# Ten transfers instead of sixteen per attention chunk, and an earlier start of attention, in a fused gated attention and MLP kernel

## The chip, the cores and the metric

The kernel runs on one core of a Trainium2 chip, as one launch. The metric is the device time of that launch in microseconds (us). PE is the matrix engine, DVE the vector engine, ACT the scalar engine, POOL the GpSimd engine and SP the engine whose queue issues the transfers (DMAs) between DRAM and on-chip memory. Every transfer of this kernel is issued from SP.

## The reference

Both branches read the same `x` (2048 rows of 512). Branch A is causal attention with 32 heads of 16 and a window of 256 keys; branch B is a dense MLP with 1792 hidden columns and tanh gelu. A sigmoid gate per row mixes them. All is float32.

```python
def _A_ref(x, wqkv, wo):
    B, S, D = x.shape
    H = 32; Dh = D // H; W = 256
    qkv = (x @ wqkv).reshape(B, S, 3, H, Dh)...      # q, k, v by head
    scores = einsum("bhqd,bhkd->bhqk", q, k) * Dh ** -0.5
    mask = (q - k >= 0) & (q - k < W)
    o = einsum("bhqk,bhkd->bhqd", softmax(where(mask, scores, -1e9)), v)
    return o.reshape(B, S, D) @ wo

def _B_ref(x, w1, b1, w2, b2):
    return gelu(x @ w1 + b1) @ w2 + b2

g = sigmoid((x * gate_w).sum(-1, keepdims=True))
out = g * a + (1 - g) * b
```

(The code is shortened; `a` and `b` are the two branches on `x`.)

## The kernel before

**Number format.** Each float32 operand is split into a high part, rounded to the narrower type `F32R`, and a low part that is the rest. A dense product is then three matmuls (high by high, high by low, low by high; `mm3`, lines 92 to 95). In attention the parts are stacked instead: one head of q or k becomes 48 partitions (16 dimensions by 3 copies), so that one matmul does the three products at once. These stacks (`ks`, `kd` for k, `qs`, `qd` for q) are why q and k go out to DRAM after the projection (tensors `SQ`, `SK`) and come back in another arrangement.

**Dense work.** The sequence is cut into four tiles of 512 rows (`T`). For each tile, `qkv` transposes x (`qkv_x`), makes eight pieces of q and k (`qkv_qk`, 128 columns, that is eight heads, each) and four of v (`qkv_v`), and stores them. After the four tiles come eight turns of the MLP (`mlp`), each on one tile and half of the hidden columns: first layer (matmuls `u`, with `gelu`), then second layer (matmuls `y`, partial sums to and from DRAM in `YA`, `YB`). Last comes `final`, the product with `wo` and the gate. While a tile of the MLP is worked on, its x is read back from `XT`.

**Attention.** Heads go in eight groups of four (`NG`), and a group in 16 blocks of 128 rows (`NKB`), four blocks to a chunk. So there are 128 block steps, 32 chunks. For step `u` the main loop (lines 785 to 812) issues, in four rounds,

- `att_max` for the block that is `LEAD` steps ahead: matmul `sm` (line 424, from `qd` and `kd`) and a row maximum on DVE (line 429);
- `att_exp`: matmul `st` (line 467, from `ks` and `qs`), the exponential on ACT (line 482), the triangular masks on POOL (lines 473, 476);
- `att_pvs` once per chunk: the matmuls `pv` with v (line 504), the sum of its two halves into the tile `nd` (lines 525, 528) and the store of `nd` to `ND` (line 529);
- `fill`: dense matmuls taken from the generator above, worth `STEP` (or `STEP0` before step 0) nanoseconds by a written cost per matmul triple.

So the dense work lies between the attention matmuls on PE, all in one order written ahead of time. `after(ns, fn)` puts a follow-up step into that order at a written delay; `need(key)` runs such steps until the key is there. Dense work worth `START` is put ahead of the first attention step.

**The loads of a chunk.** `ks`, `kd` and `qd` have two slots each and are refilled chunk by chunk: `load_qd` (four transfers, line 395), `load_kd` (one, line 387), `att_load_v` (three, lines 408 and 410), `load_ks` (six, lines 378, 379, 381) and `load_qs` (two, line 401). The first three are called at the end of the first block step of a chunk, `load_ks` at the end of the second, `load_qs` at the end of the third.

**The queue.** The orders of PE, ACT, DVE and POOL are as written. SP's order is set by the scheduling layer from the same program. SP works strictly in order: a transfer that waits for its data or for its buffer holds up all transfers behind it. Beside that, every transfer in the built program waits for the transfer eight places before it, because eight completion counters are used in turn; so at most eight are under way.

Of the kernel before, what the change touches and what calls it, by code (L numbers as in the profile page):

```python
# [32 lines left out]
def gated_mix(ctx: ExitStack, tc: tile.TileContext, x, wqkv, wo, w1, b1, w2, b2, gate_w, out):  # L33
# [90 lines left out]
    def load_raw(key, early=False):  # L124
# [15 lines left out]
        nc.sync.dma_start(raw.rearrange("p (c f) -> p c f", c=NC) if len(src.shape) == 3 else raw, src)  # L140
# [40 lines left out]
    def clear_k(i):  # L181

        pr, n = divmod(i, 2)
        for s in range(2):
            v = of_head(ks[:, pr, n], s)
            nc.scalar.activation(v, nil.unsqueeze(2).unsqueeze(3).broadcast_to([128, 4, 2, 64]), AF.Identity,
                                 bias=own[:, 2 * pr + s:2 * pr + s + 1])
# [57 lines left out]
    def qkv_qk(t, j):  # L245

        xt = xts[t]
        dst, i = (SQ[t], j) if j < NC else (SK[:, :, :, t * T:(t + 1) * T], j - NC)
# [18 lines left out]
        after(100, hi), after(700, lo)  # L267

    def qkv_v(t, b):
# [11 lines left out]
        def ev():  # L281
            to = vx[:, :, 0:16].rearrange("p (g s a) d -> p g a s d", s=2, a=2)
            for s in range(2):
                nc.scalar.activation(to[:, :, :, s], p.rearrange("p (g a s d) -> p g a s d", a=2, s=2, d=16)[:, :, :, s],
                                     AF.Copy)
            nc.sync.dma_start(SV[t][ts], vx)
# [10 lines left out]
    def qkv(t):  # L297
# [3 lines left out]
        pieces = qk[:2] + vs + qk[2:] if last else qk + vs  # L301
# [13 lines left out]
        for n, (kind, j) in enumerate(pieces):  # L315
# [17 lines left out]
            if t == 2 and n in (1, 3, 5, 7):  # L333
                clear_q(n // 2)
# [12 lines left out]
            if last and n not in (4, 5):  # L347
                load(later.pop(0))
# [15 lines left out]
    def parts(st, g_, cols):  # L364

        return st[4 * g_:4 * g_ + 4, :, :, cols].rearrange("(a s) d u c -> s (d u) a c", s=2)

    def load_ks(g_, c):


        need(("qk", c, NC + g_ // 2))
        src = parts(SK, g_, slice(c * T, (c + 1) * T))
        for pr in range(2):
            for s in range(2):
                v = f32(ks[64 * s + 4:64 * s + 52, pr, slot(g_, c)]).rearrange("r (n u j) -> r n u j", u=4, j=64)
                w = src[s, :, pr].rearrange("r (n u j) -> r n u j", u=2, j=64)
                if s:
                    nc.sync.dma_start(v[:, :, 0], w[:, :, 0])
                    nc.sync.dma_start(v[:, :, 3], w[:, :, 1])
                else:  # L380
                    nc.sync.dma_start(v[:, :, 1:3], w)

    def load_kd(g_, c):
        need(("qk", c, NC + g_ // 2))
        k0 = max(c * T - W, 0)
        src = SK[4 * g_:4 * g_ + 4, :, :, k0:(c + 1) * T].rearrange("(a s) d u c -> (s d u) a c", s=2)
        nc.sync.dma_start(f32(kd[0:96, :, slot(g_, c), k0 - c * T + W:]), src)

    def load_qd(g_, c):
        need(("qk", c, g_ // 2))  # L390
        src = parts(SQ[c], g_, slice(0, T))
        for pr in range(2):
            for s in range(2):
                v = f32(qd[48 * s:48 * s + 48, pr, slot(g_, c)]).rearrange("r (n s j) -> r n s j", s=2, j=64)[:, :, s]
                nc.sync.dma_start(v, src[s, :, pr].rearrange("r (n j) -> r n j", j=64))

    def load_qs(g_, c):
        need(("qk", c, g_ // 2))
# [464 lines left out]
```

## Time and profile before

| | |
|---|---|
| time, median of 3 runs | 806.6 us (804.92 to 808.64) |
| the profiled execution | 806.2 us, of which the span in the trace is 804.5 us |
| PE busy | 755.9 us, 94% of the span |
| PEld (weight loads, beside PE) | 616.2 us, 77% |
| DVE, ACT, POOL busy | 510.1, 432.8, 422.7 us (63%, 54%, 53%) |
| mean granted PE clock | 0.975 of full speed |
| transfers by SP's queue | 208400 packets, 174.91 MB, 78.6% of 16 DMA engines' time |

A row of waits reads: engine, line, who released it, then total us, times, and the longest. A timeline row reads: start, duration, engine, line, instruction, count, and in brackets how long the engine had been idle before and what ended that. In a row of windows, an engine's busy time is followed by its instruction count; PEclk is the clock granted to PE as a share of full speed, and it is followed by the share of the DMA engines' time that was busy and by GB/s. "SPq" is SP issuing a transfer; the transfer lands later.

### The profile page before, as it was taken

To read this page: it belongs to the slowest core of one execution; us is meant where nothing else is said; L and a number is where in the kernel's file an instruction comes from. 1 tells how busy PE (TensorE), PEld (TensorE's weight loads), DVE (VectorE), ACT (ScalarE), POOL (GpSimd) and SP (SyncE) were. 2 spreads that over 40 slices of the span, in tenths; PEclk is the share of its full clock that TensorE was granted. 3 is DMA by queue.
4 is the path that set the end of the run, shared out by engine and by line. 5 is a ranking of instruction groups with operands and counts; after the bars stand their busy time and mean duration, and the time that the engine had idled before them with its cause. 6 is when DMAs were issued, how large, how long until landed. Compare 5 with 4: busy or idle time off the path is not lost.

```text
span 804.5 us, 18387 instructions
## 1 busy us (share of the span) xinstructions
PE 755.9 (94%) x6102; PEld 616.2 (77%) x6102; DVE 510.1 (63%) x1548; ACT 432.8 (54%) x941; POOL 422.7 (53%) x1129
## 2 busy tenths in 40 slices
PE   9999999969999989989999797999978999999988
PEld 6888888848788868868777676788856887878776
DVE  4433333869579648856985597569646875793533
ACT  4434423357468427735873485458624853785541
POOL 3200000139669747856776387569844885687200
PEclk9999999989999989999999899999989999999999
DMA  9997988978977787888858888676787888758572
GB/s 301 402 332 275 358 271 268 297 155 281 213 178 188 202 201 183 241 205 185 181 145 217 229 197 238 172 175 136 216 209 174 191 232 198 184 154 250 171 245 104
DMA packets 208494, 176.09 MB, mean 219 GB/s; under 512 B 126480, under 2 KB 150288, under 8 KB 208400
## 3 DMA queue, kind: packets, MB, share of 16 engines
q1 hardware_dynamic: 208400, 174.91, 78.6%
q8 instruction: 49, 0.80, 0.5%
q14 instruction: 45, 0.37, 0.2%
HBM read 112.47 MB, written 62.39 MB: 217 GB/s over the span
## 4 chain that ended last, share of the span: by engine, by line
PE 68%; DMA 20%; DVE 5%; issue 2%; SPq 2%; POOL 1%; ACT 1%; DVEq 0%; POOLq 0%
PE pv_sm L504 7%; PE st L467 6%; PE sm L424 6%; DMA ks<-SK 6%; PE u L93 5%; PE u L95 4%; PE u L94 4%; DMA kd<-SK 4%; PE y L93 4%; PE qk L93 4%; PE qk L95 4%; PE qk L94 4%; PE y L94 4%; PE y L95 4%; DMA qd<-SQ 2%
## 5 line engine op out<-in xcount | busy, mean ns | idle before, releaser
L482 ACT ACTIVATE pt<-st 128x320 f32<-128x320 f32 (+4 forms) x512 | 207.8, 425 | 170.5 <-PE st L467 164.8
L429 DVE CUSTOM_DVE_ANT_0 jm<-sm,mask 128x320 bf16<-128x320 f32 (+4 forms) x512 | 237.5, 464 | 91.5 <-PE sm L424 67.1
L473 POOL TENSOR_SCALAR_AFFINE_SELECT pt<-pt 64x128 f32<-64x128 f32 x512 | 186.7, 365 | 178.3 <-ACT pt L482 157.1
L467 PE MATMUL st<-qs,ks 128*128 128x320 f32 (+4 forms) x512 | 159.5, 315 | 21.3 <-DMA ks<-SK 19.6
L424 PE MATMUL sm<-kd,qd 96*128 96x320 f32 (+4 forms) x512 | 158.2, 311 | 14.5 <-DMA kd<-SK 10.3
L476 POOL TENSOR_SCALAR_AFFINE_SELECT pt<-pt 64x128 f32<-64x128 f32 x448 | 152.4, 340 | 0.0
L467 PEld LDWEIGHTS st<-qs,ks 128*128 128x128 f32 x512 | 99.0, 193 | 46.8 <-issue 21.6
L424 PEld LDWEIGHTS sm<-kd,qd 96*128 96x128 f32 x512 | 98.0, 191 | 43.1 <-DVE M L429 13.5
L450 POOL CAST qs<-tt 4x512 fp32r<-4x512 f32 x128 | 90.2, 705 | 46.2 <-DVE tt L444 38.9
L95 PE MATMUL y<-w,h 128*128 128x512 f32 x224 | 89.7, 400 | 1.7 <-DVE h L619 1.7
L93 PE MATMUL y<-w,h 128*128 128x512 f32 x224 | 91.1, 407 | 0.0
L94 PE MATMUL y<-w,h 128*128 128x512 f32 x224 | 89.8, 401 | 0.0
L93 PE MATMUL u<-mx,w 128*128 128x512 f32 x196 | 81.3, 415 | 0.0
L504 PE MATMUL pv_sm<-pt,vbuf 64*32 64x320 f32 (+4 forms) x1408 | 77.5, 358 | 2.8 <-DVE M L429 2.4
L94 PE MATMUL u<-mx,w 128*128 128x512 f32 x196 | 78.2, 399 | 0.0
L95 PE MATMUL u<-mx,w 128*128 128x512 f32 x196 | 78.1, 399 | 0.0
L504 PE MATMUL pv_st<-pt,vbuf 64*32 64x320 f32 (+4 forms) x1408 | 77.0, 358 | 0.6 <-POOL pt L473 0.6
L504 PEld LDWEIGHTS pv_sm<-pt,vbuf 64*32 64x32 f32 x1408 | 53.0, 110 | 23.6 <-issue 4.0
L262 DVE TENSOR_TENSOR qke<-qk,qke 128x512 fp32r<-128x512 f32 x32 | 22.1, 691 | 49.0 <-ACT qke L259 42.8
L95 PEld LDWEIGHTS y<-w,h 128*128 128x128 f32 x224 | 43.0, 192 | 11.9 <-DVE h L619 2.1
L259 ACT ACTIVATE qke<-qk 128x512 fp32r<-128x512 f32 x32 | 19.2, 599 | 57.1 <-PE qk L95 40.1
L504 PEld LDWEIGHTS pv_st<-pt,vbuf 64*32 64x32 f32 x1408 | 49.0, 110 | 0.9 <-POOL pt L473 0.9
(140 smaller groups left out, 1330.5 us busy)
## 6 DMA issues: line engine op xcount, KB each, us to landing
kd<-SK SPq DMA_DIRECT2D x24, 576.0 KB
qd<-SQ SPq DMA_DIRECT2D x128, 96.0 KB
qs<-SQ SPq DMA_DIRECT2D x64, 192.0 KB
mx<-XT SPq DMA_DIRECT2D x24, 512.0 KB
SQ<-qke SPq DMA_DIRECT2D x16, 512.0 KB
SK<-qke SPq DMA_DIRECT2D x16, 512.0 KB
ND<-nd SPq DMA_DIRECT2D x32, 256.0 KB
raw_w<-in_B_w_dram SPq DMA_DIRECT2D x28, 256.0 KB
```

Of the source, the lines that this page charges most:

```text
L93: nc.tensor.matmul(p, lh, rh, start=first, stop=False)
L94: nc.tensor.matmul(p, lh, rl, start=False, stop=False)
L95: nc.tensor.matmul(p, ll, rh, start=False, stop=last)
L262: nc.vector.tensor_sub(e[:, 1 - h], p, f32(e[:, h]))
L424: nc.tensor.matmul(p[:, :w], qd[0:96, pr, n, 128 * j:128 * (j + 1)], kd[0:96, pr, n, k1 - w:k1], start=True, stop=True)
L429: nc.vector.tensor_tensor_reduce(junk[:, :w], p[:, :w], mask[:, 320 - w:320], 1.0, -3e38, ALU.add, ALU.max, M[:, 2 * (b % RB) + hb, pr:pr ...
L450: nc.gpsimd.tensor_copy(dst, tt[32 * i:32 * i + 4].unsqueeze(1).broadcast_to([4, 2, 2 * RB, 32]))
L467: nc.tensor.matmul(p[:, :w], ks[:, pr, slot(g_, kb // NB), at:at + 128], qs[:, pr, k0:k0 + w], start=True, stop=True)
L473: nc.gpsimd.affine_select(out=v[:, :, 0:64], in_=v[:, :, 0:64], pattern=[[0, 2], [1, 64]], compare_op=ALU.is_ge, fill=0.0, base=0, channel ...
L476: nc.gpsimd.affine_select(out=v[:, :, W:W + 64], in_=v[:, :, W:W + 64], pattern=[[0, 2], [-1, 64]], compare_op=ALU.is_ge, fill=0.0, base=- ...
L482: nc.scalar.activation(pt[:, pr, :w], p[:, :w], AF.Exp, scale=SCALE)
L504: nc.tensor.matmul(pv[r // 64][32 * i:32 * i + 32, q - c * T:e - c * T], vts[g_, b // NB][r:r + 64, v:v + 32], rhs(r), start=start, stop=s ...
```

## The change

1. **Layout in DRAM.** `SQ` and `SK` are stored as [8, 16, 3, 4, T]: the four pieces of 128 columns lie side by side, innermost but for the row. A group of four heads is now two neighbouring heads of two neighbouring pieces, and its two pairs lie side by side in DRAM and in the chip's `ks`, `qd`, `kd`. `SK` is one tensor per tile and not one for all. `SV` is stored already shifted by half a block for one of its halves.
2. **Fewer loads.** `load_ks` has 3 transfers (was 6), `load_qd` 2 (was 4), `att_load_v` 1 (was 3), `load_qs` 2 as before; `load_kd` has 2, where it was 1, for all chunks but the first of a group, since the rows of the tile before come from another tensor. That is 10 in place of 16. The stores of v are 3 per block where they were 1.
3. **Order of the loads.** `load_ks` is called one block step earlier (the first of a chunk), `load_qd`, `load_kd` and `att_load_v` one later (the second).
4. **`HOLD`.** The stores of q, k, v, `nd` and of the second layer's partial sums are put 1.5 us later in the written order than the instruction that makes their data.
5. **Start.** Attention begins after 90 us worth of dense work (was 117), in the third tile, with `LEAD` 12 (was 8); `STEP0` is 3000 (3150), `STEP` 2422 (2296). Weight loads are paced at 5 us (4). The last tile makes four q and k pieces ahead of its v pieces (two before).

```diff
-    SQ = [dr.tile([H, 16, 3, T], F32, name=f"SQ{t}") for t in range(NT)]
-    SK = dr.tile([H, 16, 3, S], F32, name="SK")
-    SV = [dr.tile([T, H, 17], F32, name=f"SV{t}") for t in range(NT)]
+    SQ = [dr.tile([H // NC, 16, 3, NC, T], F32, name=f"SQ{t}") for t in range(NT)]
+    SK = [dr.tile([H // NC, 16, 3, NC, T], F32, name=f"SK{t}") for t in range(NT)]
+    SV = [dr.tile([128, NB, 2, H // 2 * 17], F32, name=f"SV{t}") for t in range(NT)]
...
-            to = dst[8 * i:8 * i + 8].rearrange("h d s c -> (h d) s c")
+
+        def store():
+            to = dst[:, :, :, i].rearrange("h d s c -> (h d) s c")
             nc.sync.dma_start(to[:, 0:2], f32(e))
             nc.sync.dma_start(to[:, 2], f32(e[:, h]))
             done.add(("qk", t, j))
-        after(100, hi), after(700, lo)
+        after(100, hi), after(700, lo), after(700 + HOLD, store)
...
-            nc.sync.dma_start(SV[t][ts], vx)
+            nc.sync.dma_start(SV[t][:, b, 1], flat[:, n:2 * n])
+            for r in (0, 64):
+                nc.sync.dma_start(SV[t][64 - r:128 - r, b, 0], flat[r:r + 64, 0:n])
...
-            if t == 2 and n in (4, 6):
-                load_ks(0, n // 2 - 2)
-            if t == 2 and n in (9, 10):
-                load_kd(0, n - 9)
+            if t == 2 and n in (1, 2):
+                load_kd(0, n - 1)
+            if t == 2 and n in (8, 9):
+                load_ks(0, n - 8)
...
     def load_ks(g_, c):
...
+        ready(c, g_, 1)
+        n = 2 * NB
+        for s in range(2):
+            v = f32(ks[64 * s + 4:64 * s + 52, slot(g_, c)]).rearrange("r a x -> r (a x)")
+            src = part(SK[c], g_, s)
+            if s:
+                mid = v[:, 192:192 + 256 * (n - 1)].rearrange("r (n x) -> r n x", x=256)[:, :, 0:128]
+                nc.sync.dma_start(mid, src[:, 64:64 + 128 * (n - 1)].rearrange("r (n x) -> r n x", x=128))
+                ends = v.rearrange("r (n j) -> r n j", j=64)[:, 0:4 * n:4 * n - 1]
+                nc.sync.dma_start(ends, src.rearrange("r (n j) -> r n j", j=64)[:, 0:2 * n:2 * n - 1])
+            else:
+                v = v.rearrange("r (n x) -> r n x", x=256)[:, :, 64:192]
+                nc.sync.dma_start(v, src.rearrange("r (n x) -> r n x", x=128))
...
     def load_kd(g_, c):
...
+        for t in range(max(c - 1, 0), c + 1):
+            ready(t, g_, 1)
+            k0 = 0 if t == c else T - W
+            at = W if t == c else 0
+            src = heads(SK[t], g_)[:, :, :, :, k0:].rearrange("s d u a c -> (s d u) a c")
+            nc.sync.dma_start(f32(kd[0:96, slot(g_, c), :, at:at + T - k0]), src)
...
     def load_qd(g_, c):
...
+        for s in range(2):
+            v = f32(qd[48 * s:48 * s + 48, slot(g_, c)]).rearrange("r a (n s j) -> r (a n) s j", s=2, j=64)[:, :, s]
+            nc.sync.dma_start(v, part(SQ[c], g_, s).rearrange("r (n j) -> r n j", j=64))
...
     def att_load_v(g_, c):
...
-        nc.sync.dma_start(dst[:, :, 34:68], src[:, :, 68 * g_ + 34:68 * g_ + 68])
-        for r in (0, 64):
-            nc.sync.dma_start(dst[64 - r:128 - r, :, 0:34], src[r:r + 64, :, 68 * g_:68 * g_ + 34])
+        nc.sync.dma_start(dst, SV[c].rearrange("p j s c -> p (j s) c")[:, :, 34 * g_:34 * g_ + 34])
...
         def ev():
             nc.vector.tensor_add(nd, nd, pv[1])
+            after(HOLD, store)
+
+        def store():
             nc.sync.dma_start(ND[c][g_ // 2][g_ % 2], nd)
...
-        if m % NB == 0 and 0 < m < NU - NB:
+        if m % NB == (u >= 0) and NB <= m < NU - NB:
             load_qd(*divmod(m // NB + 1, NT)), load_kd(*divmod(m // NB + 1, NT))
-        if u % NB == 1 and NB < u < NU - NB:
+        if u % NB == 0 and NB <= u < NU - NB:
             load_ks(*divmod(u // NB + 1, NT))
         if u % NB == 2 and NB < u < NU - 3 * NB:
             load_qs(*divmod(u // NB + 3, NT))
-        if u % NB == 0 and u >= 0:
+        if u % NB == 1 and u >= 0:
             att_load_v(*divmod(u // NB, NT))
...
-RAWS = 150e3
+RAWS = 122e3
...
-LEAD = 8
-START = 117e3
+LEAD = 12
+QAT = 5
+START = 90e3
...
-PACE = 4000.0
+PACE = 5000.0
...
-AHEAD = 11e3
-STEP0 = 3150.0
+HOLD = 1500.0
+AHEAD = 9e3
+STEP0 = 3000.0
...
-STEP = 2296.0
+STEP = 2422.0
```

SP's order in one chunk late in the program, before. `ND<-nd` is the store of a chunk's result; `qd`, `kd` and `ks` are loads for the next chunk, `vbuf` is the load of v; `ya` and `YB` belong to the second MLP layer. A trailing x2 or x4 counts equal rows.

```order
L529 DMA ND_3_94<-nd_1_9488 128x512
L395 DMA qd<-SQ_71 48x8x64 x4
L387 DMA kd<-SK 96x2x768
L408 DMA vbuf<-SV_77 128x4x34
L410 DMA vbuf<-SV_77 64x4x34 x2
L636 DMA ya_12_9565<-YA_120 128x512
L683 DMA YB_124<-yo_10_9563 128x512
L381 DMA ks<-SK 48x4x128
L378 DMA ks<-SK 48x4x64
L379 DMA ks<-SK 48x4x64
L381 DMA ks<-SK 48x4x128
L378 DMA ks<-SK 48x4x64
```

The same chunk on SP now (the numbers of lines and buffers have moved with the code).

```order
L405 DMA ks<-SK_77 48x8x128
L400 DMA ks<-SK_77 48x7x128
L402 DMA ks<-SK_77 48x2x64
L555 DMA ND_3_97<-nd_1_9444 128x512
L419 DMA qd<-SQ_72 48x16x64 x2
L413 DMA kd<-SK_75 96x2x256
L413 DMA kd<-SK_76 96x2x512
L432 DMA vbuf<-SV_80 128x8x34
L426 DMA qs<-SQ_71 48x2x512 x2
```

The loads of `ks` stood behind the store of `nd` and seven further loads; now they stand ahead of that store. The loads of `qd` and `kd` still stand right behind it.

PE's order where attention begins, before: the first `sm` stands between two q and k pieces of the fourth tile (its x is in `xt`).

```order
L94 MATMUL qk_1_1249<-xt_942,qk_256 128x512
L95 MATMUL qk_1_1249<-xt_942,qk_256 128x512
L424 MATMUL sm_0_1_1269<-kd,qd 128x64
L93 MATMUL qk_5_1273<-xt_942,qk_280 128x512
L94 MATMUL qk_5_1273<-xt_942,qk_280 128x512
```

The same place now: the first `sm` stands in a v piece of the third tile (its x lies in `qs`), behind the third group of transposes `xp` of x for the fourth.

```order
L95 MATMUL v_0_1051<-v_452,qs 128x512
L220 MATMUL xp_2_1073<-ident,xr_2_884 128x128 x4
L93 MATMUL v_1_1082<-v_398,qs 128x512
L94 MATMUL v_1_1082<-v_398,qs 128x512
L95 MATMUL v_1_1082<-v_398,qs 128x512
L446 MATMUL sm_0_1_1089<-kd,qd 128x64
```

Between the two places lie three v pieces of the third tile, and three q and k pieces and four v pieces of the fourth.

More of the change, by code (lines that the diff above doesn't have):

```diff
@@ L300, in qkv @@
         vs = [("v", b) for b in range(NB)]
[L301 removed]
+        pieces = qk[:4] + vs + qk[4:] if last else qk + vs
         if t == 0:
@@ L346, in qkv @@
                 load_xr(t + 1)
-            if last and n not in (4, 5):
+            if last and n not in (6, 7):
                 load(later.pop(0))
@@ L383, in load_kd, with heads @@
-    def load_kd(g_, c):
[L384 to L387, printed above, removed]
-    def load_qd(g_, c):
[L390 to L395, printed above, removed]
+    def heads(st, g_):
+        return st[2 * (g_ % 4):2 * (g_ % 4) + 2, :, :, 2 * (g_ // 4):2 * (g_ // 4) + 2]
@@ L681, in y_end, with store @@
             ya_load(n * NB + b + 2)
+            def store():
+                nc.sync.dma_start((YA, YB)[half][t][ts], y)
+                done.add(("y", half, t, b))
             if n + 1 < len(TURNS):
-                nc.sync.dma_start((YA, YB)[half][t][ts], y)
+                after(HOLD, store)
             else:
                 ybs[t * NB + b] = y
-            done.add(("y", half, t, b))
+                done.add(("y", half, t, b))
         turns = [(0, i) for i in range(HF - 1)] + [(1, i) for i in range(YSWAP)] + [(0, HF - 1)]
```

68 lines of the change are left out of this document (36 added, 32 removed).

## The prediction

> **What bounds the kernel now.** I read the page first, then PE's waits, then PE's timeline for the place of each gap, then SP's timeline ahead of the gaps.
>
> ```profile
> span 804.5 us, 18387 instructions
> PE 755.9 (94%) x6102; PEld 616.2 (77%) x6102; DVE 510.1 (63%) x1548; ACT 432.8 (54%) x941; POOL 422.7 (53%) x1129
> ```
> ```profile
> PE st L467 <- DMA ks<-SK: 19.6, 14, 3.7
> PE sm L424 <- DMA kd<-SK: 10.3, 4, 6.5
> PE sm L424 <- DMA ks<-SK: 0.9, 2, 0.5
> ```
>
> PE is busy 755.9 of 804.5 us, so 48.6 us are idle. The change adds and removes no matmul, so it can only act on that idle time and on the clock. Waits for the `ks` loads are 19.6 + 0.9 = 20.5 us, for `kd` 10.3 us; no other wait of PE's is half as large. Why the loads come late is seen in one chunk, on SP and on PE.
>
> ```profile
> 656.26 0.34 SPq L529 DMA_DIRECT2D ND<-nd  x1
> 656.70 3.32 SPq L395 DMA_DIRECT2D qd<-SQ  x4
> 660.06 0.61 SPq L387 DMA_DIRECT2D kd<-SK  x1
> ...
> 663.65 0.43 SPq L381 DMA_DIRECT2D ks<-SK  x1
> 664.12 0.52 SPq L378 DMA_DIRECT2D ks<-SK  x1
> ...
> 666.97 0.44 SPq L379 DMA_DIRECT2D ks<-SK  x1
> ```
> ```profile
> 666.26 0.31 PE L424 MATMUL sm<-kd,qd 96*128 96x320 f32 x1
> 668.59 0.38 PE L467 MATMUL st<-qs,ks 128*128 128x320 f32 x1 [2.01 <-DMA ks<-SK]
> ```
> ```profile
> 664.12 4.38 DMA ks<-SK
> ```
> ```profile
> SPq L529 <- DVE nd L528: 43.3, 15, 4.8
> SPq L378 <- DMA kd<-SK: 18.0, 15, 2.3
> ```
>
> The store of `nd` (L529) stands in SP's order ahead of the loads for the next chunk and waits for DVE. SP stood 43.3 us in 15 such waits. Only after it, at 656.26, go the rest: four `qd`, `kd`, v, and the six `ks` last, from 663.65 to 667.4. One of these lands 4.38 us after its issue, at 668.50, and `st` starts at 668.59, 2.01 us late. The chunk's first `sm` at 666.26, 10.0 us after the store of `nd`, had its `kd` in time, by a load issued at 660.06. So the last loads in the queue miss their chunk. The third cause beside waiting and issuing is the limit of eight: 18.0 us of SP's waits at one `ks` transfer were for the `kd` transfer eight places ahead.
>
> **The change part by part.** The sum starts from the profiled execution: 806.2 us, that is the span of 804.5 and 1.7 around it; the median of the runs, 806.6, is 0.4 above it.
>
> *ks: three transfers, one block step earlier, ahead of the store of nd.* A chunk lasts 18 us on average (the store of `nd` repeats 32 times from 194.1 to 756.2, as its row below gives), a block step 4.5. The order shows `ks` ahead of the store, so its last issue moves from 10.7 us behind the store (666.97 against 656.26) to ahead of it, over 10 us earlier. The longest `ks` wait is 3.7 us, so all of them are covered more than twice. I take off 18.5 of 20.5 us and leave 2 for chunks where a weight load with a wait of its own stands among the `ks` loads. Bounds: 20.5 off at best; 10 if such holds are common.
>
> *The clock after these gaps.* The two longest `ks` gaps, and the granted clock in the stretch of the start and in those after `ks` gaps:
>
> ```profile
> 459.72 0.61 PE L467 MATMUL st<-qs,ks 128*128 128x320 f32 x1 [3.17 <-DMA ks<-SK]
> ```
> ```profile
> 501.49 0.41 PE L467 MATMUL st<-qs,ks 128*128 128x320 f32 x1 [3.72 <-DMA ks<-SK]
> ```
> ```profile
> 160.00:180.00 20.00, 12.95 (x54) 10.23 (x52) 13.88 (x40) 11.94 (x24) 6.09 (x12) 0.83 0.82 173
> 450.00:470.00 20.00, 15.79 (x151) 11.70 (x151) 13.52 (x37) 11.22 (x26) 8.89 (x19) 0.83 0.83 214
> 500.00:510.00 10.00, 8.51 (x120) 6.70 (x121) 2.46 (x11) 2.68 (x6) 4.03 (x11) 0.83 0.53 141
> 590.00:600.00 10.00, 8.49 (x113) 6.19 (x114) 3.34 (x12) 1.91 (x4) 3.50 (x8) 0.66 0.75 201
> 610.00:620.00 10.00, 8.12 (x117) 5.60 (x116) 5.35 (x18) 3.21 (x7) 4.20 (x9) 0.83 0.68 174
> 660.00:680.00 20.00, 17.99 (x169) 14.67 (x168) 10.47 (x39) 7.45 (x17) 10.94 (x37) 0.91 0.80 189
> ```
>
> PE's busy time there, times what the clock lacks of 1: 15.79 x 0.17 = 2.7, 8.51 x 0.17 = 1.4, 8.49 x 0.34 = 2.9, 8.12 x 0.17 = 1.4, 17.99 x 0.09 = 1.6, together 10.0 us. Some of it hangs on `kd` waits in the same stretch, so I take off 8 (bounds 4 and 10). The Trainium skill, page "TensorE: Matmul & The Clock Gate", section "Why this matters for your kernels", asks for no gap of PE over about 3 us, since one idle window halves the clock. By that rule only the gaps in the second and third of these rows and the one at the start would cost clock, and this term would be 4.1 in place of 8, the time 784. The trace does not quite agree: the stretch from 660 has one gap, of 2.01 us, and shows 0.91.
>
> *qd and kd: four transfers for five, one block step later, right behind the store of nd.* The price of one and where they land:
>
> ```profile
> L387 SPq DMA_DIRECT2D kd<-SK x32: 311/607/1344, 106.9 to 694.7; - x32
> ```
> ```profile
> L395 SPq DMA_DIRECT2D qd<-SQ x128: 537/615/2162, 122.6 to 694.1; - x128
> ```
> ```profile
> L529 SPq DMA_DIRECT2D ND<-nd x32: 319/344/1211, 194.1 to 756.2; - x32
> ```
> ```profile
> 153.02 8.74 DMA SK<-qke
> 161.77 8.35 DMA kd<-SK
> 282.30 7.27 DMA kd<-SK
> 335.95 9.45 DMA qd<-SQ
> 427.64 7.44 DMA kd<-SK
> 488.76 4.54 DMA kd<-SK
> 624.35 5.43 DMA kd<-SK
> ```
>
> Issue after the store of `nd`: 0.34 for itself, two `qd` at 0.615, two `kd` at 0.607, in all 2.8 us, where the old `kd` in the chunk above was issued 4.4 us after (0.61 + 660.06 - 656.26). `sm` needs it 10.0 us after the store. The five `kd` on the chain landed 8.35, 7.27, 7.44, 4.54 and 5.43 us after issue; 2.8 + landing - 10.0 gives 1.15, 0.07, 0.24 and twice below zero, mean 0.29 us. These are the late ones, since the chain picks them, so I take half, 0.15 us, for the 28 chunks after the start: +4 us. Below: 0, and even the 3.8 us of `kd` waits of now besides the first (10.3 - 6.5) may go. Above: the new `qd` carries twice the packets; if its issue takes twice 0.615 and it lands in the 9.45 us seen, that is the second rival.
>
> *The start.* Now the first `sm` runs at 132.8, and the first `kd` that is late follows:
>
> ```profile
> L424 PE MATMUL sm<-kd,qd x512: 193/310/603, 132.8 to 720.7; 96*128 96x320 f32 x150, 96*128 96x128 f32 x6, 96*128 96x64 f32 x5, 96*128 96x256 f32 x5
> ```
> ```profile
> 170.25 0.60 PE L424 MATMUL sm<-kd,qd 96*128 96x320 f32 x1 [6.53 <-DMA kd<-SK]
> ```
> ```profile
> 80.00:120.00 40.00, 40.00 (x185) 33.09 (x185) 12.28 (x27) 14.57 (x29) 1.23 (x8) 1.00 0.89 315
> 120.00:160.00 40.00, 40.00 (x187) 33.32 (x186) 24.10 (x79) 14.13 (x29) 2.43 (x4) 1.00 0.95 281
> ```
>
> The wait of 6.53 us comes from a store of `SK` that held its place among the eight for 8.74 us, and the `kd` load queued behind that. In the new order that load stands ahead of most of the fourth tile's stores, whose dense work is stretched by more attention steps, with weight loads every 5 us and not 4. Against that, the DMA engines are already 0.89 busy from 80 on, where the first chunks' loads now also go. I take half of the gain: 3.3 of 6.53, and 1.1 of its clock loss (12.95 x 0.17 = 2.2). Bounds: all of it, 8.7 off; or 17 more, the third rival.
>
> *What costs nothing or little.* Packets: `ks` has 48 x (7 + 2 + 8) = 816 per chunk in place of 48 x 24 = 1152, over 32 chunks 10752 fewer; the split `kd` has 4608 more (24 x 192), the `SQ` stores 2048 more, the v stores 2048 more: 1% of the 208400 fewer, and the engines are not full in the attention; 0. The 32 more v copies on ACT and 32 more v stores fall into the tiles, where ACT is busy 14.57 of 40 us; if that cover were gone, they would delay the first v load, not PE. More dense work per step and fewer steps ahead of it leave the sum of matmuls as it is. At the end, the last store of `nd` is held 1.5 us more in the order; `final` waits 2.04 us for the chain behind it:
>
> ```profile
> 777.04 0.47 PE L93 MATMUL a<-wo,ot 128*128 128x512 f32 x1 [2.04 <-DVE ao L745]
> ```
>
> I add 1 us (bounds 0 and 1.5); the trace names DVE there, but the attention result loaded just before belongs to the same chain.
>
> **The sum.** 806.2 - 18.5 - 8 + 4 - 3.3 - 1.1 + 1 = 780.3. Predicted: 780 us, 3.3% below the median. With the better bounds (20.5 + 10 + 3.8 + 8.7 off) it is 763; with the worse ones of the first two terms and no gain at the start 806.2 - 10 - 4 + 4 + 1 = 797.
>
> **The rivals.**
>
> *The gaps fill with another wait.* In the first layer's stretches DVE is nearly full:
>
> ```profile
> 380.00:420.00 40.00, 37.47 (x331) 30.10 (x330) 36.66 (x103) 31.81 (x69) 29.80 (x75) 1.00 0.73 167
> ```
>
> DVE is busy 36.66 of 40 us there, 92%, and PE 37.47. If a `ks` gap goes, PE asks for `sm`'s row maxima sooner and finds DVE behind. Against: the longest `ks` gaps, at 501 and 668, lie where DVE is slack (2.46 of 10 from 500, 10.47 of 20 from 660), and the larger `STEP` thins the row maxima. If half of the two `ks` terms is lost this way (13 us), it is 793.
>
> *kd and qd take the place of ks: slower.* The place is the first `sm` of each of 28 chunks, with two block steps of cover for the loads instead of three. The saved terms are 18.5 + 8 + 3.4 (the start less the end) = 29.9 us, so it turns slower where the mean wait passes 29.9 / 28 = 1.07 us, that is where `kd` lands on average later than 10.0 - 2.8 + 1.07 = 8.3 us after issue. The worst of the five above was 8.35, a `qd` took 9.45, and the new `qd` ahead of it has twice the packets. At 8.8 us the wait is 1.6 us, 28 times 45, and the time 806.2 - 29.9 + 45 = 821. Against it: the six `ks` transfers that now crowd behind `kd` are by then done, and three of the five landed within 7.4 us.
>
> *The start costs what the rest gains.* If each of the first three chunk starts waits as the one at 170 did, with its clock, it is 3 x 8.7 = 26.1 in place of 8.7 us: 806.2 - 18.5 - 8 + 4 + 1 + 17.4 = 802. For it speak the 0.89 and 0.95 of the DMA share; against it that these loads are no more bytes in all.
>
> *Better than forecast.* If `kd` waits vanish and the start is clean: about 766.
>
> **How the numbers follow.** Forecast (770 to 790) 0.52; DVE fills the gaps (793) 0.13; the start (802) 0.08; `kd` and `qd` late (821) 0.18; better (766) 0.09. A measurement of this kernel can tell about 0.5%, 4 us, from no change, so "same" runs from 803 to 811. Faster: 0.52 + 0.13 + 0.09 = 0.74. The start's case lies at the edge: 0.07 of it goes to same, 0.01 to slower, with the 0.18 of late `kd`: 0.19. The range is 762 to 806: it holds the forecast, DVE's case, the start's case and the better bounds, and leaves out the 0.18 and about 0.02 below.
>
> **What would show it.** Right: `st` waiting for `ks` under 3 us in all; `sm` waiting for `kd` or `qd` some 4 to 10 us; PE idle near 28 us; the clock above 0.98; on SP, `ks` issued ahead of the store of `nd`. Wrong: a wait of `sm` of over 1 us in most chunks (late `kd`), DVE as the releaser of PE in the first layer's stretches (the first rival), or PE idle of over 15 us between 90 and 170 (the start).

## The result, and the profile after

The changed kernel takes 812.24 us (median of 20 runs; 806.96 to 819.99), the kernel before in the same sessions 804.46 (799.68 to 809.89); 780 was predicted. The ratio is 1.0086, 95% interval 1.0059 to 1.0112: slower by 0.9%. This ratio and those below leave out runs over 1.5% above the fastest of their kernel, while the medians hold all runs. The profiled execution took 816.4 us, 4.2 above the median; its span is 814.7, and the clock was 0.969 (0.975 before).

The head of the page after:

```profile
span 814.7 us, 18155 instructions
PE 755.1 (93%) x6102; PEld 618.5 (76%) x6102; DVE 511.1 (63%) x1548; ACT 432.2 (53%) x973; POOL 425.6 (52%) x1129
```

PE is as busy as before (755.9). Its idle time went from 48.6 to 59.6 us, 11.0 more, and with 0.8 us less of busy time the span is 10.2 us longer. PE's waits after (engine, line, releaser, total us, times, longest):

```profile
PE sm L446 <- DMA kd<-SK: 26.8, 11, 7.8
PE sm L446 <- DMA vbuf<-SV: 9.7, 1, 9.7
PE sm L446 <- DMA qs<-SQ: 4.0, 2, 2.9
PE sm L446 <- DVE M L451: 3.7, 7, 2.0
PE sm L446 <- DMA OT<-num: 1.7, 1, 1.7
PE st L490 <- ACT pt L505: 1.3, 1, 1.3
```

The 20.5 us of waits for `ks` are gone: `st` has one wait left, for ACT. But `sm` now waits 26.8 + 9.7 + 4.0 + 1.7 = 42.2 us for loads, 10.3 + 0.9 before. The releaser is the transfer that came last by the profile; all of these waits stand at the first `sm` of a chunk. The four longest gaps on PE's timeline (start, duration, instruction, idle before):

```profile
175.07 0.39 PE L446 MATMUL sm<-kd,qd 96*128 96x64 f32 x1 [7.81 <-DMA kd<-SK]
223.01 0.60 PE L446 MATMUL sm<-kd,qd 96*128 96x320 f32 x1 [9.71 <-DMA vbuf<-SV]
298.95 0.38 PE L446 MATMUL sm<-kd,qd 96*128 96x320 f32 x1 [4.01 <-DMA kd<-SK]
375.28 0.60 PE L446 MATMUL sm<-kd,qd 96*128 96x320 f32 x1 [4.76 <-DMA kd<-SK]
```

SP ahead of the last of these, from the store of `nd` on, and the landing of `kd` on the chain (the profile's chain of work that ended last; start of the issue, us to landing):

```profile
360.57 0.34 SPq L555 DMA_DIRECT2D ND<-nd  x1
361.01 1.82 SPq L590 DMA_DIRECT2D mx<-XT  x4
362.87 0.80 SPq L419 DMA_DIRECT2D qd<-SQ  x1
363.72 1.43 SPq L413 DMA_DIRECT2D kd<-SK  x2
```
```profile
364.40 10.75 DMA kd<-SK
```

`sm` asked at 375.28 - 4.76 = 370.52, 9.95 us after the store of `nd`, where the prediction had 10.0. The last `kd` was issued 3.8 us after the store (364.40), behind four transfers of the MLP's next x (`mx`, 512 KB each), and landed after 10.75 us: 3.8 + 10.75 - 9.95 = 4.6, and 0.13 us behind the landing make the gap. The prediction had 2.8 us, but counted the last issue whole; to its start, where the landing begins to count, its own prices give 2.2.

Ahead of the longest gap, at 223.01, SP also stood at `mx` itself, for the stores of the tile that it reads back:

```profile
SPq L590 <- DMA XT<-xt: 5.0, 2, 3.5
```

One `qd` and both `kd` stood behind it, so that the last `kd` went out 11.0 us after the store of `nd` (213.08 against 202.03).

Landings of `kd` on the chain, first at the wait from 167 to 175, then in later chunks:

```profile
164.43 10.39 DMA kd<-SK
288.28 10.58 DMA kd<-SK
483.33 7.63 DMA kd<-SK
```

All nine on the chain (with those of 146.38, 364.40, 521.64, 617.75, 635.03 and 672.52: 5.86, 10.75, 9.15, 6.33, 8.28, 6.96) have a mean of 8.4 us, the five of before 6.6. They are transfers of 384 KB, behind one of 192 KB in all chunks but the first of a group; before, it was one of 576 KB. The granted clock (PE busy, PEld, DVE, ACT, POOL, then PEclk):

```profile
160.00:180.00 20.00, 12.19 (x70) 9.95 (x76) 9.38 (x33) 8.75 (x20) 8.65 (x27) 0.76 0.95 214
220.00:230.00 10.00, 6.99 (x108) 5.22 (x108) 2.81 (x10) 1.31 (x3) 3.46 (x8) 0.58 0.67 110
600.00:610.00 10.00, 8.58 (x109) 6.35 (x115) 4.86 (x20) 2.19 (x5) 3.53 (x11) 0.66 0.76 170
```

The clock is low in stretches with gaps, as before; only the gaps lie elsewhere. Beside the changes listed above, the four pieces of `wo` come in four transfers each, where it was one.

### The profile page after: what moved, and what is told of

The parts are those of the page before. It is cut to its first block, busy times and chain, and to the rows that moved or that the text cites. A ratio compares the mean times of both kernels' runs of the same rounds, so it can differ in the third digit from the quotient of the medians.

```text
span 814.7 us, 18155 instructions
## 1 busy us (share of the span) xinstructions
PE 755.1 (93%) x6102; PEld 618.5 (76%) x6102; DVE 511.1 (63%) x1548; ACT 432.2 (53%) x973; POOL 425.6 (52%) x1129
## 2 busy tenths in 40 slices
DMA packets 203949, 176.06 MB, mean 216 GB/s; under 512 B 102480, under 2 KB 145744, under 8 KB 203856
## 3 DMA queue, kind: packets, MB, share of 16 engines
q1 hardware_dynamic: 203856, 174.90, 80.3%
## 4 chain that ended last, share of the span: by engine, by line
PE 53%; DMA 18%; DVE 5%; SPq 4%; issue 3%; ACT 3%; POOL 2%; POOLq 0%; DVEq 0%; ACTq 0%
DMA kd<-SK 9%; PE sm L446 6%; PE pv_sm L527 6%; PE st L490 6%; PE y L93 4%; PE u L93 4%; PE u L94 4%; PE u L95 4%; PE y L94 4%; PE y L95 4%; DVE jm L451 2%; PE a L93 2%; PE a L95 2%; PE a L94 2%; DMA vbuf<-SV 2%
## 5 line engine op out<-in xcount | busy, mean ns | idle before, releaser
L496 POOL TENSOR_SCALAR_AFFINE_SELECT pt<-pt 64x128 f32<-64x128 f32 x512 | 188.1, 367 | 206.7 <-ACT pt L505 186.5
L446 PE MATMUL sm<-kd,qd 96*128 96x320 f32 (+4 forms) x512 | 159.8, 314 | 47.3 <-DMA kd<-SK 26.8
L499 POOL TENSOR_SCALAR_AFFINE_SELECT pt<-pt 64x128 f32<-64x128 f32 x448 | 156.8, 350 | 0.0
L473 POOL CAST qs<-tt 4x512 fp32r<-4x512 f32 x128 | 87.5, 684 | 38.6 <-DVE tt L467 19.3
L93 PE MATMUL y<-w,h 128*128 128x512 f32 x224 | 94.3, 421 | 0.0
L94 PE MATMUL y<-w,h 128*128 128x512 f32 x224 | 90.7, 405 | 0.0
L95 PE MATMUL y<-w,h 128*128 128x512 f32 x224 | 90.4, 404 | 0.0
L93 PE MATMUL u<-mx,w 128*128 128x512 f32 x196 | 79.3, 405 | 0.0
L94 PE MATMUL u<-mx,w 128*128 128x512 f32 x196 | 78.0, 398 | 0.0
L95 PE MATMUL u<-mx,w 128*128 128x512 f32 x196 | 77.5, 395 | 0.0
L551 DVE TENSOR_TENSOR nd<-nd,pv_sm 128x512 f32<-128x512 f32 x32 | 21.9, 685 | 45.5 <-ACT nd L548 42.4
```

Source lines behind the costliest of these rows:

```text
L93: nc.tensor.matmul(p, lh, rh, start=first, stop=False)
L94: nc.tensor.matmul(p, lh, rl, start=False, stop=False)
L95: nc.tensor.matmul(p, ll, rh, start=False, stop=last)
L446: nc.tensor.matmul(p[:, :w], qd[0:96, n, pr, 128 * j:128 * (j + 1)], kd[0:96, n, pr, k1 - w:k1], start=True, stop=True)
L473: nc.gpsimd.tensor_copy(dst, tt[32 * i:32 * i + 4].unsqueeze(1).broadcast_to([4, 2, 2 * RB, 32]))
L496: nc.gpsimd.affine_select(out=v[:, :, 0:64], in_=v[:, :, 0:64], pattern=[[0, 2], [1, 64]], compare_op=ALU.is_ge, fill=0.0, base=0, channel ...
```

## Experiments

The theory after the result: `kd` and `qd`, asked for one block step later, have too little cover for the time they take to land. Rivals: their place behind the store of `nd` is the cause; the new numbers are; the smaller number of transfers gives nothing; and DVE fills whatever gap is closed. Ratios are to the kernel before in the same session, with 95% intervals. The median of the kernel before moved between 803.29 and 806.16 us over these sessions, so differences between two experiments are good to some 3 us at best.

### The call of qd and kd

The changed kernel, with `qd` and `kd` asked for a step earlier (`m` counts blocks of `sm`):

```diff
-        if m % NB == (u >= 0) and NB <= m < NU - NB:
+        if m % NB == 0 and NB <= m < NU - NB:
             load_qd(...), load_kd(...)
```

> The changed kernel with one edit: load_qd and load_kd are called at the first block step of a chunk, as before the change, so that in SP's order they stand ahead of the store of nd, together with ks. Theory 1 (the gaps moved from st/ks to sm/kd, because the qd and kd loads stand behind the store of nd and whatever else waits there, with two block steps of cover): the 42 us in which sm waits for loads fall below 12, ks waits stay under 4, and the time falls to 780 to 792 us. Theory 2 (ten larger transfers land later whatever their place): sm keeps waiting over 25 us and the time stays within 805 to 815. Theory 3 (the new pacing of dense work and attention is what costs): the time stays above 803, with waits in other places.

794.49 us, ratio 0.988 (0.981 to 0.995); span 791.6, PE busy 747.7, clock 0.986. PE's waits, and SP in one chunk:

```profile
PE st L490 <- DMA ks<-SK: 8.9, 9, 1.6
PE sm L446 <- DVE M L451: 6.7, 10, 2.2
PE pv_st L527 <- DMA vbuf<-SV: 5.9, 3, 2.7
PE sm L446 <- DMA kd<-SK: 3.7, 4, 1.9
```
```profile
337.81 0.53 SPq L419 DMA_DIRECT2D qd<-SQ  x1
338.38 1.03 SPq L413 DMA_DIRECT2D kd<-SK  x2
339.50 1.13 SPq L405 DMA_DIRECT2D ks<-SK  x1
...
345.36 0.34 SPq L555 DMA_DIRECT2D ND<-nd  x1
345.80 1.81 SPq L590 DMA_DIRECT2D mx<-XT  x4
```

One line turns 0.9% slower into 1.2% faster. `kd` now goes 7 us ahead of the store of `nd` and of `mx`, and its waits fall from 26.8 to 3.7 us. Of the 23.1 us by which the span is shorter than after, 15.7 are idle time and 7.4 PE's busy time, at the better clock. The waits for `ks`, 8.9 us at `st` and 1.6 at `sm`, stay above the 4 expected. The counterpart is the kernel before with nothing but the new call order:

```diff
-        if m % NB == 0 and 0 < m < NU - NB:            # qd, kd
+        if m % NB == (u >= 0) and NB <= m < NU - NB:
-        if u % NB == 1 and NB < u < NU - NB:           # ks
+        if u % NB == 0 and NB <= u < NU - NB:
-        if u % NB == 0 and u >= 0:                     # v
+        if u % NB == 1 and u >= 0:
```

> The kernel before with one part of the change alone: ks is called at the first block step of a chunk, qd, kd and v at the second; sixteen transfers, old layout, old numbers, no hold. Theory 1 (call order decides who is late): the ks waits fall from 20.5 to under 5 us and sm's waits for kd and qd rise from 10 to 30 or more; time 800 to 815. Theory 2 (the larger transfers are what makes kd late): kd waits stay near 10 us and the time falls below 795.

819.41 us, ratio 1.018 (1.011 to 1.024). The call order alone costs more than the whole change:

```profile
PE sm L424 <- DMA kd<-SK: 45.7, 15, 6.6
```

No wait for `ks` is left of 20.5 us, and those for `kd` grew from 10.3 to 45.7. Next, what stands ahead of them in the queue. First the next x (`mx`) put behind `qd`, `kd` and v:

```diff
-            load_x(TURNS[n + 1][1], f"mx{half}")
+            pend.append((TURNS[n + 1][1], f"mx{half}"))
...
+            while pend:                                # behind att_load_v
+                load_x(*pend.pop(0))
```

> The changed kernel with one edit: the reload of a tile's x for the MLP (four transfers of 512 KB, mx) is put behind the next kd and v loads in the written order instead of where the first layer's turn ends. In the changed kernel's trace three of the longest waits of sm (9.7, 4.0 and 4.8 us) follow a kd load that stands right behind mx. Theory 1a (that collision is a main part of the loss): those three gaps go, PE idle falls by 15 to 20 us and the time by about as much plus 3 to 5 us of clock, to 790 to 797. Theory 1b (the place behind the store of nd costs in every chunk, mx only picks which): the kd waits spread to other chunks and the time stays within 804 to 812.

800.03 us, ratio 0.992 (0.989 to 0.996): 12 us come back, by the place of six groups of four transfers. The result lies between the two theories: the three long gaps behind `mx` are gone, but other chunks now wait, the longest 6.6 us, and `sm` still waits 29.1 us for loads (42.2 before this edit). The first late `kd`, ahead of any `mx`, keeps its 7.2 us. Of 19.4 us by which the span is shorter, only 8.1 are idle time (15 to 20 were expected); 11.3 are PE's busy time. Then the store of `nd`, held 6 us so that the loads go ahead of it (`NORM` 0 lets the normalization follow it at once):

```diff
-            after(HOLD, store)
+            after(6000.0, store)
...
-NORM = 4500
+NORM = 0
```

> The changed kernel with the store of nd held 6 us and not 1.5 (and att_norm called at once after it, so that it comes 0.5 us later than before); qd, kd and v are still called at the second block step but now stand ahead of that store on SP. If the place behind the store is the cause: sm's waits for loads fall from 42 to under 20 us and the time to 790 to 800. If the shorter cover is the cause: the waits stay above 28 us and the time within 803 to 815.

812.73 us, ratio 1.013 (1.008 to 1.018); `sm` still waits 24.2 us for `kd` and 9.2 for v. This run alone does not clear the place, for SP now stood 55.7 us at the load of `den`, for the store ahead of it to land (8.3 in the changed kernel). And the changed kernel with the early call and without the hold, so that the store goes out as soon as before:

```diff
 # on the kernel with qd and kd a step earlier
-HOLD = 1500.0
+HOLD = 0.0
```

> The changed kernel with qd and kd called at the first block step and HOLD 0, so that the store of nd stands ahead of kd and ks again on SP, while all of them are called in one step. Theory 1 in its strict form (what stands behind the store of nd is late): kd and ks waits of over 15 us, time 800 to 808. If three block steps of cover are enough even behind that store: within 4 us of the first experiment, 791 to 798.

796.86 us, ratio 0.992 (0.987 to 0.996), not told apart from 794.49, though `kd` now goes out behind the store (328.37 against 327.99 in one chunk) and SP stands longer at that store (84.1 us, 17.3 with the hold). `sm` waits 5.7 us for `kd`, `st` 12.5 for `ks`. So the place behind the store alone is not the cause. The block step is, and what of the bulk transfers stands ahead.

### Fewer transfers

The kernel with the early call, its chunk loads cut again into pieces (6 `ks`, 4 `qd`, 3 v, 2 `kd`, 2 `qs`):

```diff
-            nc.sync.dma_start(mid, ...)      # ks: three transfers, both pairs at once
-            nc.sync.dma_start(ends, ...)
-            nc.sync.dma_start(v, ...)
+        for pr in range(2):                   # three for each pair; qd per pair;
+            ...                               # v in three pieces
```

> The kernel of the first experiment (qd and kd at the first step, new numbers, 794.5 us) with the transfers of a chunk cut up again: six ks, four qd, three v, two kd, two qs, the same bytes from the same new layout, with the old packet sizes in ks. If the number of transfers is of no weight once they stand in time: 792 to 797. If the eight under way and SP's issue time count: 800 to 812, with ks waits above 15 us.

811.72 us, ratio 1.007 (1.003 to 1.011).

```profile
PE pv_st L531 <- DMA vbuf<-SV: 13.3, 7, 4.4
PE sm L450 <- DVE M L455: 7.8, 10, 1.6
PE pv_sm L531 <- DVE M L455: 5.7, 4, 2.8
```

With the loads called in time, the ten transfers are worth some 16 us (17 by the medians, 15.5 by the ratios). The pieces are also smaller: SP's queue moved 218192 packets in place of 203856, so the number of transfers and that of packets are not told apart. Part shows as waits, though not for `ks` as expected: v 13.3 instead of 5.9, DVE 13.5 instead of 9.0. PE was also busy 758.1 us (747.7) at a clock of 0.981; that is more than the clock explains, and stays open.

### Does DVE fill the gaps?

The kernel before with `ks` alone asked for a step earlier:

```diff
-        if u % NB == 1 and NB < u < NU - NB:
+        if u % NB == 0 and NB <= u < NU - NB:
             load_ks(...)
```

> The kernel before with one edit: ks called at the first block step too, right behind qd and kd and ahead of v; sixteen transfers, old numbers, no hold, all of it behind the store of nd. If the number of transfers hardly matters (the place does): ks waits fall from 20.5 to under 8 us and kd waits stay near 10, time 790 to 797, a ratio as of the first experiment. If the transfers must be few for this to work: kd or ks waits stay over 20 us together and the time is above 800.

806.29 us, ratio 1.006 (1.003 to 1.010). PE's waits, then DVE's:

```profile
PE pv_sm L504 <- DVE M L429: 14.8, 5, 4.1
PE sm L424 <- DMA kd<-SK: 9.8, 7, 5.5
PE sm L424 <- DVE M L429: 5.1, 9, 1.3
PE st L467 <- DMA ks<-SK: 1.9, 6, 0.7
```
```profile
DVE den L543 <- DMA den<-ND: 34.6, 12, 6.9
```

The `ks` waits are nearly gone and nothing is gained: PE waits 19.9 us for DVE's row maxima in their place (4.8 before). DVE is not full; it works in order and stands at `den` (line 543), the normalization's reciprocal, whose load is late (34.6 us, 24.2 before). Behind that stand the row maxima. One such place, DVE and then PE:

```profile
295.04 0.35 DVE L543 RECIPROCAL den<-den 128x32 f32<-128x32 f32 x1 [5.40 <-DMA den<-ND]
295.31 0.43 DVE L429 CUSTOM_DVE_ANT_0 jm<-sm,mask 128x320 bf16<-128x320 f32 x1
```
```profile
295.80 0.42 PE L504 MATMUL pv_sm<-pt,vbuf 64*32 64x64 f32 x2 [3.63 <-DVE M L429]
```

To see whether that can be delayed away, the normalization's three steps on DVE were put later in the order, on this kernel:

```diff
-        after(6000, rcp), after(10500, back), after(17000, mul)
+        after(9500, rcp), after(14000, back), after(23000, mul)
```

> The kernel of the sixth experiment (the one before with ks called at the first block step; 806 us though sm and st then waited only 11.7 us for loads) with the longer delays of att_norm. There DVE waited 34.6 us for den and 9.8 for rb, and PE 19.9 us for DVE M. If that took the place of the ks waits: DVE M falls below 8 us and the time to 785 to 796, with sixteen transfers and the old numbers. If not: 802 to 808.

827.67 us, ratio 1.030 (1.026 to 1.034). The expectation failed: the wait moved to the product `num` by `rb`, where DVE stood 61.1 us, and `sm` waited 29.5 us for the row maxima.

### The new numbers

The old numbers on the changed kernel, and then on the one with the early call:

```diff
-RAWS, LEAD, QAT, START = 122e3, 12, 5, 90e3
-PACE, AHEAD, STEP0, STEP = 5000.0, 9e3, 3000.0, 2422.0
+RAWS, LEAD, QAT, START = 150e3, 8, 1, 117e3
+PACE, AHEAD, STEP0, STEP = 4000.0, 11e3, 3150.0, 2296.0
```

> The changed kernel with the old schedule numbers (START 117, LEAD 8, STEP 2296, STEP0 3150, PACE 4, AHEAD 11; qs loads from step 1): new layout, new transfers, new call order and HOLD alone. Theory 1: sm still waits for kd in many chunks, 15 to 30 us in all, but with mx falling elsewhere the longest gaps are gone: 795 to 805. Theory 2: 808 or more. Theory 3 (the numbers cost): below 790.

817.93 us, ratio 1.016 (1.010 to 1.022), with 34.7 us of waits for `kd`: the new numbers help, if anything, even while `kd` is late, so they are not what made the change slow.

> The changed kernel with qd and kd called at the first block step and the old schedule numbers (START 117, LEAD 8, STEP 2296, STEP0 3150, PACE 4, AHEAD 11). It tells what the new numbers are worth with the loads in time. If nothing: 791 to 797 as with the new ones. If the new numbers help as the third experiment against the changed kernel suggests: 797 to 803. If they cost: below 789.

808.86 us, ratio 1.004 (1.001 to 1.008). PE, and DVE:

```profile
PE sm L446 <- DVE M L451: 24.9, 12, 8.8
```
```profile
DVE num L579 <- DMA rb<-RD: 29.5, 8, 9.9
```

With the loads in time, the old numbers cost some 14 us, more than expected: DVE stands at `num`, PE behind it. The norm's steps put later by the same edit as above, in this kernel:

> The kernel of the seventh experiment (changed kernel, qd and kd at the first step, old schedule numbers; 808.9 us, PE waiting 24.9 us for DVE M, DVE 29.5 us for rb) with the longer delays of att_norm. If the old numbers are slow only because they put att_norm's loads late: 785 to 796, near the new numbers. If the numbers matter by themselves: above 800.

799.17 us, ratio 0.992 (0.988 to 0.996). The waits for DVE's maxima fell to 1.2 us, but `pv` waited 17.0 us for v, whose load stood behind those of `num` and `rb` at five of the six longest of these waits; 9.7 us remain as a gain. Which number it is, three single steps on the kernel with the early call. The pace of the weight loads:

```diff
-PACE = 5000.0
+PACE = 4000.0
-RAWS = 122e3
+RAWS = 150e3
```

> The kernel of the first experiment (794.5 us) with the old pace of the weight loads alone (PACE 4 us, RAWS 150). If the pace is what the old numbers lost (SP waits 31.7 us for DVE's weight splits there, 18.7 here): 800 to 809 and DVE M waits above 15 us. If START, LEAD and STEP are: 791 to 797.

789.10 us, ratio 0.981 (0.976 to 0.987): not the pace, and rather better than expected. The start and the lead:

```diff
-START = 90e3
+START = 102e3
-LEAD = 12
+LEAD = 8
-QAT = 5
+QAT = 1
```

> The changed kernel with qd and kd in the first block step, and three of the old numbers (START 102, LEAD 8, QAT 1) beside the new STEP and STEP0. With all the old numbers but the pace the kernel lost some 15 us to waits of DVE for the norm's loads. If the step between chunks (STEP, STEP0) is what keeps DVE from them, this stays at 789 to 797 us and sm waits for DVE under 10 us; if an early start and a long lead are what bring them, it goes to 800 to 809 us with 15 us or more of them.

794.19 us, ratio 0.990 (0.983 to 0.996), 9.6 us of waits for the maxima: not the lead, and not the earlier start as far as 102. The dense work per block step, with `START` raised so that the sum of the work stays:

```diff
-STEP = 2422.0
+STEP = 2296.0
-START = 90e3
+START = 106e3
```

> The changed kernel with qd and kd in the first block step, and the old STEP of 2296 (in place of 2422) with START raised to 106 so that the dense work ahead of attention and in it adds up as before; LEAD 12 and the rest stay new. The run with START 102, LEAD 8 and QAT 1 stayed at 794 us with under 10 us of waits of sm for DVE, so these are not what the old numbers cost. If the thinner step is, this goes to 800 to 809 us with 15 us or more of waits of sm and pv for DVE. If it stays at 790 to 797 us with under 12 us of them, it is not STEP alone either, but STEP0, AHEAD, RAWS or several together.

812.01 us, ratio 1.010 (1.006 to 1.013).

```profile
PE 760.0 (94%) x6102; PEld 620.7 (77%) x6102; DVE 510.3 (63%) x1548; ACT 431.1 (53%) x973; POOL 417.0 (51%) x1129
```
```profile
PE sm L446 <- DVE M L451: 14.2, 9, 6.2
PE sm L446 <- DMA kd<-SK: 8.3, 3, 4.7
```

It is `STEP`, with the `START` that goes with it: 5% less dense work in a block step costs 17.5 us. (`START` of 106 alone, `STEP0` and `AHEAD` were not tried by themselves.) In the two profiled executions 7.0 us of the 19.3 are idle time, spread over DVE, `kd` and POOL and not on DVE alone, as I had expected; 12.3 are PE's busy time at a clock of 0.962.

### The repairs together

The two edits in one kernel, the early call of `qd` and `kd` and `mx` behind the loads:

```diff
-        if m % NB == (u >= 0) and NB <= m < NU - NB:
+        if m % NB == 0 and NB <= m < NU - NB:
...
-            load_x(TURNS[n + 1][1], f"mx{half}")
+            pend.append((TURNS[n + 1][1], f"mx{half}"))
```

> The changed kernel with both edits of the first two experiments: qd and kd called at the first block step, mx behind the next v loads. If the two repair different gaps (theory 1 with the mx collision beside it): 783 to 790, the waits of pv for v (5.9 us in the first of them) shrink, since XT, mx stood ahead of v there. If they repair the same gaps: 792 to 797.

790.68 us, ratio 0.984 (0.976 to 0.991), between the two expectations and within the error of 794.49. The same with the norm later:

```diff
-        after(6000, rcp), after(10500, back), after(17000, mul)
+        after(9500, rcp), after(14000, back), after(23000, mul)
```

> The kernel of the fifth experiment (qd and kd at the first block step, mx behind v) with one edit: the three delays of att_norm are longer (9.5, 14 and 23 us for 6, 10.5 and 17), so that its reciprocal and product stand later in DVE's order. In that kernel's trace DVE stands 16.5 us before the reciprocal until den has come from DRAM and 5.7 us before the product until rb has; the row maxima queued behind wait too, and PE waits for those (DVE M, 9.6 us). If DVE's order is what now holds PE: DVE's waits for den and rb fall below 5 us, PE's waits for DVE M below 5, time 780 to 787. If those waits are harmless: 788 to 793.

795.75 us, ratio 0.991 (0.988 to 0.994). It missed both expectations: PE's waits for the maxima fell to 2.3 us, but 13.5 for v came, and DVE's waits for `den` and `rb` stayed at 21.6 us (22.2 without the delays). And with the old pace in place of that:

```diff
-PACE, RAWS = 5000.0, 122e3
+PACE, RAWS = 4000.0, 150e3
```

> The changed kernel with qd and kd asked for in the first of a group's three block steps, the next blocks' x behind them, and the old pace (PACE 4, RAWS 150). My theory: the loads are then all in time and the old pace does no harm, so the two repairs add up in part: the span falls from 786 to about 784, the time to 785 to 789 us, with less than 10 us of waits of sm and st for loads. If the place of x and the pace serve the same few transfers, it stays at 789 to 791 us.

787.33 us, ratio 0.978 (0.973 to 0.982), the best of all. Its gain over its two parts is within their error. Its page and PE's waits:

```profile
span 781.2 us, 18190 instructions
PE 744.9 (95%) x6102; PEld 612.3 (78%) x6102; DVE 512.0 (66%) x1548; ACT 432.9 (55%) x973; POOL 421.0 (54%) x1129
```
```profile
PE sm L446 <- DMA kd<-SK: 4.5, 3, 2.3
PE sm L446 <- DVE M L451: 4.2, 7, 2.2
PE st L490 <- DMA ks<-SK: 3.9, 5, 1.0
```

## Why the prediction was wrong

**The waits for ks: right.** 20.5 us were there, 18.5 were forecast to go, all went.

**qd and kd: the step that failed.** It was sized at +4 us, "I take half, 0.15 us, for the 28 chunks". The loads of `sm` after the start cost 42.2 - 8.9 (the start: 7.81 at 175.07 and 1.1 at 152.51) = 33.3 us, 1.2 us for each of the 28 chunks. The wait is where it was forecast, at the first `sm` of a chunk, which came 9.95 us after the store of `nd` in the chunk shown. Three things were not as forecast.

What stands ahead: I counted two `qd`, but in three of the six chunks where the MLP turns to its next x, `mx` stands between the store and `kd`. These three have the gaps of 9.71, 4.01 and 4.76 us, 18.5 of the 33.3. There `mx` held SP for 5.0 us in one chunk and took 1.8 us of issuing in the one shown above, and then moved 2 MB on the same engines. My two order pieces showed a chunk without it.

The issue: in the 27 chunks from 183 on, by SP's timeline, the last `kd` went out 0.9 to 11.0 us after the store, 3.9 on average, where my sum has 2.2 to the same point. A single issue was not dearer (`qd` 0.46 us, `kd` 0.68, the medians); waits and other transfers come between.

The landing: 6.3 to 10.75 us after the start (8.4 is the mean of all nine), where I had 4.5 to 8.35 and halved the excess, since the chain picks late loads. Without the halving the term would still have been only 0.29 x 28 = 8 us.

The rival that I gave 0.18 had the mechanism. That the figures meet its threshold (a landing of 8.3 us, a wait of 1.07; 8.4 and 1.2 were measured) is in part luck: 8.4 is a mean of loads that the chain picks, only 12 of the 28 chunks have such a wait of over 0.25 us, and the threshold set 29.9 us of savings against the waits, of which 24.3 came (20.5 for `ks`, 3.8 for the `kd` waits of before). The early call removes these waits, and the call order alone brings them into the kernel before; that is shown.

**The clock: its 8 us were not saved.** The stretches with a low clock hold gaps, and there is more idle time after (59.6 us) than before (48.6). In the best kernel, where PE idles 36.3 us and not 48.6, the saving is there: PE's busy time is 744.9 us, 11.0 less than before, at a clock of 0.987. But it does not go by idle time alone: with `mx` behind the loads PE idles 51.5 us and is busy only 743.8. How the clock follows from the gaps stays open. The Trainium skill, "TensorE: Matmul & The Clock Gate", section "Why this matters for your kernels", asks only that no gap exceed some 3 us; the stretch from 600 to 610 after, whose gaps are 1.42 us and, just ahead of it, 1.98, shows a clock of 0.66. Here the measurement decides: gaps of under 2 us can be paid for too.

**The start: failed.** I took half of 6.53 us off. The wait became 7.81 + 1.1 us, and the clock loss 12.19 x 0.24 = 2.9 in place of 2.2. The load that was late before, the third chunk's, did come ahead of most of the fourth tile's stores, at 127.11, and nothing waits for it. But two later loads took its place:

```profile
127.11 2.09 SPq L413 DMA_DIRECT2D kd<-SK  x2
145.81 1.03 SPq L413 DMA_DIRECT2D kd<-SK  x2
164.43 2.00 SPq L413 DMA_DIRECT2D kd<-SK  x1
```

The last of them, for the second group's first chunk, stands behind seven of the eight pairs of q and k stores of that tile, and took 10.39 us to land while the DMA engines were 0.95 busy. With the early call the stretch from 100 to 180 has 4.2 us of idle PE instead of 9.2.

**The sum, measured.** Idle time: 20.5 less for `ks`, 3.8 less for the `kd` waits of before beside the first, 33.3 more for the loads of `sm`, 8.9 - 6.5 = 2.4 more at the start, together +11.4; -0.4 in all else makes the +11.0 of the two pages. With 0.8 us less of busy PE the span is 10.2 us longer. The end, priced at +1, is in all else: the wait ahead of `final` was 1.07 us, 2.04 before.

**DVE fills the gaps: not in the changed kernel, but real.** The waits for row maxima were 4.2 us after and 4.8 before. In the kernel before with only the `ks` wait removed, though, and in the changed one with the early call and the old numbers, it took what was won (19.9 and 25.1 us). I had read "DVE 92% busy" as the cause; the traces show DVE standing idle for a late load of the normalization with the maxima behind it. So even had `qd` and `kd` cost the forecast +4, what the `ks` term gains seems to depend on the larger `STEP`, to which I gave no price.

## What to carry to other kernels

When one queue issues all loads in order, a new order of calls changes the cover of each of them: price the one that ends with the least by the slow landings seen, and list all that can stand ahead of it at its new place, with its own waits, in the worst chunk and not in a clean one. A closed wait is worth its time only if the engine that is next late has room; here the ten transfers (some 16 us) and a thicker step (17.5 us) each paid only beside the other, and one call in the wrong step (some 17 us) hid both. Before putting a step that waits for a load later in an engine's order, look at which load its own transfers then delay.

## What the runs showed of the hardware

PE's busy time is no constant: with the same 6102 matmuls it ran from 743.8 to 761.9 us over these kernels. Its product with the mean clock moves less: 755.9 x 0.975 = 737 before, 755.1 x 0.969 = 732 after, 744.9 x 0.987 = 735 in the best, and 730 to 738 in all of them but the one with the loads cut into pieces (758.1 x 0.981 = 744). A `kd` transfer of 384 KB landed 5.9 to 10.75 us after its issue in the nine cases on the chain after the change: 10.6 and 10.75 behind 2 MB of `mx`, and 10.4 at the start, behind most of a tile's stores.
